# Attention, MLP and experts on one core: the first six attention groups in another order, with part of the first loads on ScalarE's DMA queue

## Chip, core and metric

The kernel runs on one core of a Trainium2 chip. The metric is device time in microseconds of one execution. The core has five engines that run their own instruction streams in order: TensorE (PE, with its weight loads PEld), VectorE (DVE), ScalarE (ACT), GpSimd (POOL) and SyncE (SP). DMAs are issued by an instruction on an engine's queue and carried out by 16 DMA engines; an engine that needs the data waits for a semaphore that the DMA raises when it has landed.

## What is computed

```python
# q, k, v: (2, 8, 576, 64); heads 0-3 local, heads 4-7 strided, stride 32
scores = np.where(mask, scale * q @ k.T, -1e9)
attn = softmax(scores)                     # row maximum taken off, sum + 1e-9
x = (attn @ v) -> (1152, 512)              # heads side by side
h = np.maximum(x @ w_in, 0.0)              # w_in (512, 2048)
x = h * h @ w_out                          # w_out (2048, 512)
p = domain_probs / (domain_probs.sum(-1, keepdims=True) + 1e-9)
out = sum(p[:, e:e+1] * (np.maximum(x @ w1[e], 0.0) @ w2[e]) for e in range(4))
```

## The kernel before

The work is cut into tasks: a DMA, a run of matmuls, one elementwise step. `Plan.add` records each with the engines that may run it and an estimated cost, the tasks it follows, the buffers that it takes and frees, and a rank. `Plan.run` then plays the tasks through a small model: whenever an engine is idle it takes the ready task of lowest rank, and the instructions are written out in the order of the model's start times. This order is fixed in the program; the hardware only waits on semaphores. Where TensorE would have nothing to do before a set point, the model puts in filler matmuls (128x512 on a zero tile, line 1395).

The attention is done in groups: `Strided(b, j)` (three per batch) and `Local(b, j)` (five per batch). `attend` (line 499) makes a group's tasks: loads of k, q and v; the scores, S (lines 404 to 408 and 471 to 479); row maximum, difference, Exp on ScalarE (line 537, or 531 for small groups), row sum, reciprocal, normalisation on GpSimd (line 541); four transposes, T (413, 483); a copy of them to SBUF on ScalarE (line 521); the values product, V (425, 493); and the split of the result into a high and a low part (ScalarE line 551, VectorE line 555) in the x tiles, which the MLP reads. T0, V0, T1 and so on name these steps of the group that comes first, second, ... in time on TensorE. Six groups of batch 0 (the list `startup`) stand at the start; the other ten are spread between MLP products later. V3 is the values product of the first `Local` group, the fourth.

The MLP's weights come as 8-byte words of which two 4-byte halves are fetched as `raw` (512 KB each) and put together on ScalarE (mid, line 695), VectorE (shift 698, low half 703), and split into a high part on ScalarE (line 709) and a low part on GpSimd or VectorE (line 713). The MLP's products (lines 732 to 734) are three matmuls of 384 columns each; the first of them needs x of the three strided groups and the first half of the first weight unit.

All loads are issued by SyncE, in the model's order. Tiles: k, q, v, p (probabilities), pt (their transposes), st (row statistics), raw, mid, val, w (weights); ba, bh, by are PSUM banks. `cb` holds masks and an identity in bf16 and is read by the first score matmul, `ident` (read from `ci`) by the transposes. The framework gives each DMA, whatever queue it is on, one of eight completion semaphores (DMAHW0 to DMAHW7) in turn, in the program's order, and makes it wait for the semaphore's previous DMA where that isn't known to be done.

Of the kernel before, what the change touches and what calls it, by code (L numbers as in the profile page):

```python
# [10 lines left out]
U32 = mybir.dt.uint32  # L11
# [57 lines left out]
class Plan:  # L69
# [10 lines left out]
    warm = 6900  # L80
# [23 lines left out]
    def run(self):  # L104
# [7 lines left out]
        ready = {"pe": [], "act": [], "dve": [], "pool": [], "dma": [], "none": []}  # L112
# [13 lines left out]
        while done < len(self.tasks):  # L126
# [4 lines left out]
            while events and events[0][0] == now:  # L131
# [6 lines left out]
                elif what == "end":  # L138
# [7 lines left out]
                    for y in then.get(t, ()):  # L146
                        waits[y] -= 1
                        lag = 0 if y.behind is t else self.DMA if t.ran == "dma" else self.SAME if t.ran in y.engines else self.CROSS
# [3 lines left out]
            for e in ready:  # L152
                while idle[e] and ready[e]:
# [21 lines left out]
                    got.end = now + got.engines[e] * (2 if e == "pe" and now < self.warm else 1)  # L175
                    order.append((now, len(order), got.emit, e))
# [18 lines left out]
def tile_attention_mlp_experts(ctx: ExitStack, tc: tile.TileContext, a, out):  # L195
# [24 lines left out]
    HOLD = 5500  # L220
    EACH = 3169
    AHEAD = 2080
    END2 = 13621
    END3 = 9597
    CONV0 = 7564
    CONV = 113841
# [5 lines left out]
    BASE = 3308  # L232
    R_MAX = 232
    R_EXP = 219
    R_NORM = 708
# [3 lines left out]
    R_LO = 383  # L239
    R_OUT = 2681  # L240
    GROUP = 4
    NRAW = 3
# [6 lines left out]
    LEAD0, LEAD = 8230, 2552  # L249
# [41 lines left out]
    def mm_r(n):  # L291
        return int(n / 2.4) + 13
# [13 lines left out]
    def dma(nbytes):  # L306
        return int(nbytes / 310) + 60
# [39 lines left out]
    t_cb = plan.add({"dma": dma(P * CB * 2)}, lambda e: nc.sync.dma_start(out=cb, in_=a["cb"]), rank=-10000)  # L347
    t_go = plan.add({"none": HOLD}, lambda e: None)
    t_ci = plan.add({"dma": dma(P * P * 4)}, lambda e: nc.sync.dma_start(out=ident, in_=a["ci"]), rank=4500)
# [21 lines left out]
    class Strided:  # L371
        def __init__(self, b, j):
# [6 lines left out]
            self.cost_s = mm_r(U * n) + 2 * U * packed(n, n)  # L379
# [12 lines left out]
        def load(self, env, what):  # L392
            b, n, c = self.b, self.n, self.r0 * 2 * NM
            if what == "k":
                nc.sync.dma_start(out=env["k"][:, : U * n], in_=a["ks"][b, :, c : c + U * n])
            elif what == "q":
                nc.sync.dma_start(out=env["q"][:, : U * n], in_=a["qs"][b, :, c : c + U * n])
            else:
                nc.sync.dma_start(out=env["v"], in_=a["vs"][b, self.j])
# [38 lines left out]
    class Local:  # L438
# [19 lines left out]
        def load(self, env, what):  # L458
            b, t0, nq = self.b, self.t0, self.nq
            if what == "k":  # L460
                nc.sync.dma_start(out=env["k"][:, : 2 * (STRIDE + nq)].rearrange("p (t c) -> p t c", t=2), in_=a["kl"][b, :, :, t0 : t0 + STRIDE + nq])
            elif what == "q":
                nc.sync.dma_start(out=env["q"][:, : 2 * nq], in_=a["ql"][b, :, 2 * t0 : 2 * (t0 + nq)])
# [1021 lines left out]
```

## Time and profile before

| what | us |
|---|---|
| median of 3 runs (625.24 to 626.15) | 625.48 |
| the profiled execution | 624.48 |
| its span, first to last instruction | 622.7 |
| TensorE busy in the span | 613.6 |

The profile is of one execution. A timeline row gives start, duration, engine, line, operation, and in brackets the idle time before it and what ended it. A windows row gives each engine's busy time in a stretch, the granted TensorE clock as a share of full speed (PEclk), the mean busy share of the 16 DMA engines and what they moved.

### The profile page before, as it was taken

What the parts mean: (1) busy time and instruction counts of PE and PEld (TensorE: products, weight loads), DVE (VectorE), ACT (ScalarE), POOL (GpSimd) and SP (SyncE); (2) the same over time, 40 slices, a digit from 0 to 9 for tenths busy, and PEclk for the clock granted to TensorE, in tenths of its full rate; (3) what the DMA queues carried; (4) which work ended last, traced back from release to release, by engine and by line L of the source; (5) the groups of instructions that cost most, each with busy time, mean ns of one, the idle gap of its engine ahead of it and who ended that gap; (6) DMA issues with size and microseconds to landing.
All of it is one profiled execution on the core that took longest, in us unless ns stands there. A gap on an engine that the chain in (4) does not pass through costs nothing.

```text
span 622.7 us, 10098 instructions
## 1 busy us (share of the span) xinstructions
PE 613.6 (99%) x3742; PEld 559.8 (90%) x3742; DVE 458.0 (74%) x883; ACT 298.9 (48%) x697; POOL 149.8 (24%) x170
## 2 busy tenths in 40 slices
PE   8999999999999999999999999999999999999997
PEld 4798999999899999999898989899898989898996
DVE  4688777887687994597767585867876775978654
ACT  2967684555453643475454444534444534444330
POOL 2332012544021101023223231404132231314000
PEclk9899999999999999999999999999999999999999
DMA  8977521122212200002030203020120302030012
GB/s 265 304 212 224 162 74 65 34 75 95 102 68 68 68 1 1 17 24 63 17 85 18 84 18 85 18 63 23 47 55 18 85 17 85 17 85 1 1 51 102
DMA packets 37441, 45.14 MB, mean 72 GB/s; under 512 B 4688, under 2 KB 26640, under 8 KB 37392
## 3 DMA queue, kind: packets, MB, share of 16 engines
q1 hardware_dynamic: 37392, 44.50, 23.4%
q8 instruction: 29, 0.48, 0.3%
q14 instruction: 20, 0.16, 0.1%
HBM read 42.13 MB, written 2.36 MB: 71 GB/s over the span
## 4 chain that ended last, share of the span: by engine, by line
PE 85%; DVE 8%; ACT 2%; issue 2%; DMA 2%; SPq 1%; DVEq 0%; ACTq 0%
PE by L1247 11%; PE by L1246 11%; PE by L1248 10%; PE bh L732 10%; PE bh L733 10%; PE bh L734 10%; PE by L732 3%; PE by L734 3%; PE by L733 3%; PE ba L732 3%; PE ba L733 3%; PE ba L734 3%; DVE r L971 1%; PE ba L479 1%; DMA raw<-in_wi_dram 1%
## 5 line engine op out<-in xcount | busy, mean ns | idle before, releaser
L1199 DVE SCALAR_TENSOR_TENSOR acc<-by,pe,acc 128x512 f32<-128x512 f32 (+1 forms) x109 | 79.2, 742 | 24.5 <-PE by L1248 24.2
L732 PE MATMUL bh<-x,w 128*128 128x384 f32 x240 | 82.8, 345 | 0.7 <-DVE h L1271 0.4
L733 PE MATMUL bh<-x,w 128*128 128x384 f32 x240 | 80.6, 336 | 0.2 <-DVE x L767 0.2
L734 PE MATMUL bh<-x,w 128*128 128x384 f32 x240 | 80.5, 336 | 0.0
L1144 POOL TENSOR_TENSOR sf<-raw,raw 128x256 f32<-128x256 f32 x40 | 32.0, 804 | 183.6 <-DMA raw<-in_w_dram 133.2
L1155 ACT ACTIVATE w<-sf 128x256 fp32r<-128x256 f32 x110 | 43.4, 409 | 50.6 <-POOL sf L1144 50.6
L1247 PE MATMUL by<-o,h 128*128 128x512 f32 (+1 forms) x134 | 52.4, 391 | 0.0
L1246 PE MATMUL by<-o,h 128*128 128x512 f32 (+1 forms) x134 | 52.1, 389 | 0.0
L1248 PE MATMUL by<-o,h 128*128 128x512 f32 (+1 forms) x134 | 51.8, 386 | 0.0
L732 PE MATMUL by<-h,w 128*128 128x384 f32 x144 | 49.7, 345 | 1.0 <-ACT acc L837 1.0
L732 PEld LDWEIGHTS bh<-x,w 128*128 128x128 f32 x240 | 45.2, 188 | 4.0 <-DVE r L1366 1.1
L734 PE MATMUL by<-h,w 128*128 128x384 f32 x144 | 48.3, 335 | 0.0
L733 PE MATMUL by<-h,w 128*128 128x384 f32 x144 | 48.2, 335 | 0.0
L733 PEld LDWEIGHTS bh<-x,w 128*128 128x128 f32 x240 | 45.2, 188 | 1.0 <-DVE x L767 0.5
L734 PEld LDWEIGHTS bh<-x,w 128*128 128x128 f32 x240 | 45.1, 188 | 0.0
L1144 POOL TENSOR_TENSOR sf<-sf,raw 128x256 f32<-128x256 f32 x40 | 32.3, 817 | 22.4 <-DVE w L1163 22.2
L733 PE MATMUL bh<-w,w 128*128 128x384 f32 x110 | 37.0, 336 | 0.0
L734 PE MATMUL bh<-w,w 128*128 128x384 f32 x110 | 36.9, 336 | 0.0
L732 PE MATMUL bh<-w,w 128*128 128x384 f32 x110 | 36.9, 335 | 0.0
L1179 DVE TENSOR_TENSOR o<-raw,o 128x512 fp32r<-128x512 f32 x30 | 21.1, 706 | 21.3 <-ACT o L1176 21.3
L1176 ACT ACTIVATE o<-raw 128x512 fp32r<-128x512 f32 x30 | 18.8, 631 | 35.9 <-PE by L1248 35.5
L1366 DVE TENSOR_TENSOR r<-r,bh 128x384 f32<-128x384 f32 x49 | 26.9, 550 | 11.4 <-ACT r L1361 7.1
(268 smaller groups left out, 1627.9 us busy)
## 6 DMA issues: line engine op xcount, KB each, us to landing
raw<-in_wi_dram SPq DMA_DIRECT2D x16, 512.0 KB, 3.9
raw<-in_wo_dram SPq DMA_DIRECT2D x16, 512.0 KB, 3.9
raw<-in_w_dram SPq DMA_DIRECT2D x64, 128.0 KB, 2.7
raw<-in_w_dram SPq DMA_DIRECT2D x32, 256.0 KB, 2.8
out_dram<-acc SPq DMA_DIRECT2D x8, 256.0 KB, 2.0
v<-in_vs_dram SPq DMA_DIRECT2D x6, 256.0 KB, 4.4
v<-in_vl_dram SPq DMA_DIRECT2D x8, 192.0 KB, 4.1
k<-in_kl_dram SPq DMA_DIRECT2D x8, 160.0 KB, 4.1
```

Of the source, the lines that this page charges most:

```text
L732: nc.tensor.matmul(dst, lhsT=wh, rhs=xh, start=start, stop=False, skip_group_check=again)
L733: nc.tensor.matmul(dst, lhsT=wh, rhs=xl, start=False, stop=False, skip_group_check=again)
L734: nc.tensor.matmul(dst, lhsT=wl, rhs=xh, start=False, stop=stop, skip_group_check=again)
L1144: nc.gpsimd.tensor_tensor(out=value(dst), in0=value(x), in1=value(y), op=ALU.subtract if n in MINUS else ALU.add)
L1155: nc.scalar.activation(out=op_slot(env["op"])[:, 0].rearrange("p k f -> p (k f)"), in_=value(src), func=AF.Copy, scale=float(sign))
L1176: nc.scalar.activation(out=late[env["w2"]][:, 0], in_=f32(raws[f]["raw"][:, DM:]), func=AF.Copy)
L1179: nc.vector.tensor_tensor(out=late[env["w2"]][:, 1], in0=f32(raws[f]["raw"][:, DM:]), in1=f32(late[env["w2"]][:, 0]), op=ALU.subtract)
L1199: nc.vector.scalar_tensor_tensor(out=acc, in0=o, scalar=pcol, in1=acc, op0=ALU.mult, op1=ALU.add)
L1246: nc.tensor.matmul(o, lhsT=h[:, 0, ts], rhs=w[:, 0], start=new, stop=False)
L1247: nc.tensor.matmul(o, lhsT=h[:, 0, ts], rhs=w[:, 1], start=False, stop=False)
L1248: nc.tensor.matmul(o, lhsT=h[:, 1, ts], rhs=w[:, 0], start=False, stop=stop)
L1366: nc.vector.tensor_tensor(out=at_(), in0=at_(), in1=bank["bank"][:, :TB], op=ALU.add if sign > 0 else ALU.subtract)
```

## The change

DMAs may now stand on a second queue, "dma2", issued by ScalarE (`nc.scalar.dma_start`); the model lets the two queues share the rate, and all "dma2" tasks are written out at time 0. On it go `cb`, `ident`, the v of the first six groups and the first two raw weight tiles; all other loads stay on SyncE. The six groups have ranks of their own (FIRST, LKQ, LV), and for them the copy of the transposes, the high part of the result and the normalisation may also run on VectorE; the high part of the first weight units may too. The first four MLP products have ranks of their own (EARLY_H) and may use the banks `by`. Some constants of the planner are other numbers.

```diff
-    warm = 6900
+    warm = 5300
...
-                    order.append((now, len(order), got.emit, e))
+                    other = {"dma": "dma2", "dma2": "dma"}.get(e)
+                    slow = now < self.warm if e == "pe" else other and (ready[other] or not idle[other])
+                    got.end = now + got.engines[e] * (2 if slow else 1)
+                    order.append((0 if e == "dma2" else now, len(order), got.emit, e))
...
-    HOLD = 5500
-    EACH = 3169
+    HOLD = 4721
...
+    FIRST = (-15498, -14603, 1146, 17685, 23706, 17552)
+    LKQ = (-9194, -10361, -8349, -7854, -7681, -7609)
+    LV = (-9957, -8431, -7025, -8031, -5968, -3705)
...
+    AHEAD_H = 4
+    EARLY_H = (-14744, -12844, 22108, 24008), (-6663, -4763, 42744, 44644), (21457, 23357, 48317, 50217), (-34452, -32552, 21056, 22956)
...
+    QUEUE2 = (("wi", 0, 1), ("wi", 0, 0))
...
-    t_cb = plan.add({"dma": dma(P * CB * 2)}, lambda e: nc.sync.dma_start(out=cb, in_=a["cb"]), rank=-10000)
+    t_cb = plan.add({"dma2": dma(P * CB * 2)}, lambda e: nc.scalar.dma_start(out=cb, in_=a["cb"]), rank=-10000)
...
-            loads.append(plan.add({"dma": dma(nbytes)}, lambda e, w=what: g.load(env, w), rank=rank - lead, take=[(env, what, [what])]))
+            loads.append(plan.add({"dma2" if early is not None and what == "v" else "dma": dma(nbytes)}, lambda e, w=what: g.load(env, w, nc.scalar if e == "dma2" else nc.sync), rank=(LV if what == "v" else LKQ)[early] if early is not None else rank - lead, take=[(env, what, [what])]))
...
-        t = plan.add({"pool": norm(n)}, lambda e: eng[e].tensor_tensor(out=view(env["p"]), in0=view(env["p"]), in1=wide(1), op=ALU.mult), after=[t], rank=rank + R_NORM, free=[(env, "st")])
+        t = plan.add({"pool": norm(n), "dve": dve(n)} if early is not None else {"pool": norm(n)}, lambda e: eng[e].tensor_tensor(out=view(env["p"]), in0=view(env["p"]), in1=wide(1), op=ALU.mult), port=True, after=[t], rank=rank + R_NORM, free=[(env, "st")])
...
-        t = plan.add({"act": act(g.npt)}, copy, after=[t], rank=rank + R_T + 500, take=[(env, "pt", ["pt"])], free=[(env, "T")])
+        t = plan.add({"act": act(g.npt), "dve": dve(g.npt)} if early is not None else {"act": act(g.npt)}, copy, after=[t], rank=rank + r_t + 500, take=[(env, "pt", ["pt"])], free=[(env, "T")])
...
-            t = plan.add({"act": act(cols)}, hi, after=[t_v], rank=rank + R_X)
+            t = plan.add({"act": act(cols), "dve": dve(cols)} if early is not None else {"act": act(cols)}, hi, after=[t_v], rank=rank + r_x)
...
-        attend(g, BASE + EACH * k, ["bank_a", "bank_y"], LEAD0)
+        attend(g, FIRST[k], ["bank_a", "bank_y"], 0, k, WHOLE[k])
...
-                chain["dma"] = plan.add({"dma": dma(P * 4 * CH * 4)}, load, after=[chain["dma"]], rank=rank - FETCH, take=[(env, "raw", ["raw"])])
+                chain["dma"] = plan.add({"dma2" if (kind, c, j) in QUEUE2 else "dma": dma(P * 4 * CH * 4)}, load, after=[chain["dma"]], rank=LW.get((kind, c, j), rank - FETCH), take=[(env, "raw", ["raw"])])
```

What this makes of the program's order at three places (names as in the code, with buffer numbers; the sizes are partitions x elements).

SyncE's first DMAs before:

```order
L347 DMA cb<-in_cb_dram 128x410
L395 DMA k_115<-in_ks_dram 128x432
L397 DMA q_111<-in_qs_dram 128x432
L399 DMA v_119<-in_vs_dram 128x512
L395 DMA k_116<-in_ks_dram 128x432
L397 DMA q_112<-in_qs_dram 128x432
L399 DMA v_120<-in_vs_dram 128x512
L395 DMA k_117<-in_ks_dram 128x288
L397 DMA q_113<-in_qs_dram 128x288 [waits DMAHW0_49]
L399 DMA v_121<-in_vs_dram 128x512 [waits DMAHW1_49]
L349 DMA ident<-in_ci_dram 128x128 [waits DMAHW2_49]
```

And after, on the same queue, with the semaphores that each waits for:

```order
L407 DMA k_115<-in_ks_dram 128x432
L409 DMA q_111<-in_qs_dram 128x432
L407 DMA k_116<-in_ks_dram 128x432
L409 DMA q_112<-in_qs_dram 128x432
L407 DMA k_117<-in_ks_dram 128x288
L409 DMA q_113<-in_qs_dram 128x288 [waits DMAHW1_49]
L473 DMA k_118<-in_kl_dram 128x2x160 [waits DMAHW3_49]
L475 DMA q_114<-in_ql_dram 128x256 [waits DMAHW5_49]
```

SyncE has k and q alone at the start; the second strided group's now come first. ScalarE's queue before, from its start:

```order
L537 ACT_TABLE_LOAD
L537 ACTIVATE p_125<-p_125 128x8x54 [waits DVE_49]
L537 ACTIVATE p_126<-p_126 128x8x54 [waits DVE_49]
L537 ACTIVATE p_127<-p_127 128x8x36 [waits DVE_49]
L521 ACTIVATE pt_130<-by_108 128x512 [waits PE_49]
```

And after, from its start:

```order
L411 DMA v_119<-in_vs_dram 128x512
L708 DMA raw_90<-in_wi_dram 128x1024
L361 DMA ident<-in_ci_dram 128x128 [waits DMAHW0_49]
L411 DMA v_120<-in_vs_dram 128x512 [waits DMAHW2_49]
L708 DMA raw_91<-in_wi_dram 128x1024 [waits DMAHW4_49]
L477 DMA v_121<-in_vl_dram 96x512 [waits DMAHW7_49]
L411 DMA v_122<-in_vs_dram 128x512 [waits DMAHW1_49]
L477 DMA v_123<-in_vl_dram 96x512 [waits DMAHW2_49]
L477 DMA v_124<-in_vl_dram 96x512 [waits DMAHW3_49]
L550 ACT_TABLE_LOAD
L550 ACTIVATE p_125<-p_125 128x8x54 [waits DVE_49]
L714 ACTIVATE mid_93<-raw_90 128x512
```

The DMA of `cb` stands ahead of these, without a wait. The ten DMAs stand ahead of the table load and the first Exp. VectorE before, from its first row maximum (L526) on:

```order
L526 TENSOR_REDUCE st_132<-ba_105 128x8
L536 TENSOR_TENSOR p_125<-ba_105,st_132 128x8x54
L526 TENSOR_REDUCE st_133<-ba_106 128x8
L536 TENSOR_TENSOR p_126<-ba_106,st_133 128x8x54
L538 TENSOR_REDUCE st_132<-p_125 128x8
```

And after:

```order
L539 TENSOR_REDUCE st_132<-ba_105 128x8
L549 TENSOR_TENSOR p_125<-ba_105,st_132 128x8x54
L551 TENSOR_REDUCE st_132<-p_125 128x8
L717 TENSOR_SCALAR val_95<-mid_93 128x512
L552 TENSOR_SCALAR st_132<-st_132 128x8
L722 SCALAR_TENSOR_TENSOR val_95<-raw_90,val_95 128x512
L539 TENSOR_REDUCE st_133<-ba_106 128x8
L553 RECIPROCAL st_132<-st_132 128x8
L549 TENSOR_TENSOR p_126<-ba_106,st_133 128x8x54
```

The sum of the first group's Exps (L538 before, L551 after) and two steps of the first weight's conversion now stand ahead of the second group's maximum. On TensorE the first MLP products stand earlier among the attention steps, right behind V3 and one set of transposes:

```order
L505 MATMUL ba_105<-pt_131,v_121 64x64 x8
L495 MATMUL by_107<-ident,p_129 96x128 x4
L754 MATMUL bh_103<-x_75,w_80 128x384
L755 MATMUL bh_103<-x_75,w_80 128x384
L756 MATMUL bh_103<-x_75,w_80 128x384
L754 MATMUL bh_104<-x_75,w_80 128x384
```

Before, a score and two sets of transposes stood there, and the MLP products were taken one at a time. From the matmul after the last attention group's values product on, both kernels have the same order on TensorE.

## Rows read from the trace of the kernel before

**Rows 1.** The page, part 1: busy us (share of span), instructions.
```profile
PE 613.6 (99%) x3742; PEld 559.8 (90%) x3742; DVE 458.0 (74%) x883; ACT 298.9 (48%) x697; POOL 149.8 (24%) x170
```
**Rows 2.** Windows: length, busy us by engine (instructions), PEclk, DMA share, GB/s.
```profile
100.00:150.00 50.00, 49.90 (x297) 49.51 (x294) 41.19 (x63) 25.86 (x53) 23.10 (x19) 1.00 0.20 64
```
**Rows 3.** TensorE's timeline: start us, duration us, operation, idle before and releaser.
```profile
5.65 0.57 PE L404 MATMUL ba<-cb 128*128 128x432 bf16 x1
...
11.28 0.88 PE L479 MATMUL ba<-k,q 64*64 64x96 f32 x16 [1.07 <-DMA q<-in_ql_dram]
...
14.30 0.60 PE L413 MATMUL by<-ident,p 128*128 128x128 f32 x4
...
15.17 0.60 PE L413 MATMUL by<-ident,p 128*128 128x128 f32 x4
...
21.69 0.69 PE L493 MATMUL by<-pt,v 96*64 96x64 f32 x16
23.22 0.38 PE L474 MATMUL ba<-cb 128*128 128x384 bf16 x1 [0.84 <-DVE x L555]
...
26.60 0.50 PE L732 MATMUL bh<-x,w 128*128 128x384 f32 x1
...
99.66 0.69 PE L493 MATMUL ba<-pt,v 96*64 96x64 f32 x16
```
**Rows 4.** Windows, the stretch of the lower clock.
```profile
23.35:26.76 3.41, 3.41 (x26) 2.94 (x26) 2.56 (x10) 2.68 (x8) 2.06 (x2) 0.50 1.04 408
```
**Rows 5.** ScalarE's timeline.
```profile
0.73 1.28 ACT L537 ACT_TABLE_LOAD   x1 [0.73 <-PEq L1474]
8.61 0.56 ACT L537 ACTIVATE p<-p 128x432 f32<-128x432 f32 x1 [6.59 <-DVE p L536]
...
15.63 0.68 ACT L695 ACTIVATE mid<-raw 128x512 f32<-128x512 f32 x1
```
**Rows 6.** SyncE's DMA issues in its timeline.
```profile
1.18 0.42 SPq L395 DMA_DIRECT2D k<-in_ks_dram  x1
...
3.06 0.43 SPq L397 DMA_DIRECT2D q<-in_qs_dram  x1
...
7.72 0.34 SPq L465 DMA_DIRECT2D v<-in_vl_dram  x1
```
**Rows 7.** SyncE's waits: total us, times, longest.
```profile
SPq L465 <- DMA q<-in_qs_dram: 0.5, 1, 0.5
```
**Rows 8.** Windows, the rate of the loads (the last two numbers of a row).
```profile
0.00:5.00 5.00, 4.01 (x10) 1.49 (x11) 0.11 (x1) 1.28 (x1) 2.57 (x9) 1.00 0.56 165
5.00:10.00 5.00, 4.54 (x104) 2.92 (x101) 2.23 (x4) 0.56 (x1) 0.00 (x0) 1.00 0.98 321
10.00:15.00 5.00, 3.93 (x46) 2.57 (x45) 3.79 (x15) 1.07 (x3) 1.78 (x2) 1.00 1.07 307
...
25.00:30.00 5.00, 5.00 (x58) 4.25 (x57) 3.48 (x12) 4.06 (x17) 1.41 (x2) 0.82 1.03 393
```
**Rows 9.** The chain of waits, first 30 us: start, us from issue to landing.
```profile
3.06 4.64 DMA q<-in_qs_dram
...
10.16 5.46 DMA raw<-in_wi_dram
```
**Rows 10.** The tile k, first 30 us: its twelve DMAs.
```profile
DMA to landing us min/median/max: 2.8/4.1/6.0
```
**Rows 11.** VectorE's timeline: difference, sum, and a weight's shift and low half.
```profile
9.59 0.61 DVE L536 TENSOR_TENSOR p<-ba,st 128x432 f32<-128x432 f32 x1
10.12 0.59 DVE L538 TENSOR_REDUCE st<-p 128x8 f32<-128x432 f32 x1
...
16.34 0.43 DVE L698 TENSOR_SCALAR val<-mid 128x512 uint32<-128x512 uint32 x1 [1.02 <-ACT mid L695]
16.80 0.69 DVE L703 SCALAR_TENSOR_TENSOR val<-raw,val 128x512 uint32<-128x512 uint32 x1
```
**Rows 12.** GpSimd's timeline: the normalisations of the first two groups.
```profile
11.92 1.78 POOL L541 TENSOR_TENSOR p<-p,st 128x432 f32<-128x432 f32 x2 [8.82 <-DVE st L539]
```

More of the change, by code (lines that the diff above doesn't have):

```diff
@@ L147, in run @@
                         waits[y] -= 1
-                        lag = 0 if y.behind is t else self.DMA if t.ran == "dma" else self.SAME if t.ran in y.engines else self.CROSS
+                        lag = 0 if y.behind is t else self.DMA if t.ran in ("dma", "dma2") else self.SAME if t.ran in y.engines else self.CROSS
                         ready_at[y] = max(ready_at.get(y, 0), now + lag)
@@ L500, in tile_attention_mlp_experts, with attend @@
     attention_done, transposed = [], []
-    def attend(g, rank, rings, lead):
+    def attend(g, rank, rings, lead, early=None, whole=False):
         env = {}
+        r_t, r_v, r_x = ((S_T, S_V, S_X) if g.kk == (2, 3) else (L_T, L_V, L_X)) if early is not None else (R_T, R_V, R_X)
         n = g.units * g.cols
@@ L526, in attend @@
         t = plan.add({"dve": dve(n)}, lambda e: nc.vector.tensor_reduce(out=stat(0), in_=view(env["S"], g.cols), op=ALU.max, axis=AX.X), after=[t], rank=rank + R_MAX, take=[(env, "st", ["st"])])
-        if g.units <= 4:
+        if g.units <= 4 and not whole:
             def each(e):
@@ L680, in tile_attention_mlp_experts @@
         wide_ = kind in ("wi", "wo")
-        soon = wide_ and first[u] <= LAG
-        rank = when[u] - (CONV0 if soon else CONV2 if not wide_ else CONV if c <= half // 2 else CONV1)
+        soon = wide_ and c == 0
+        rank = when[u] - (CONV2 if not wide_ else CONV if c <= half // 2 else CONV1)
+        late_ = rank
         for j in (1, 0) if kind == "wi" else (0, 1):
+            rank = EARLY.get((kind, c, j), late_) if wide_ else late_
             env = {} if wide_ or j == 0 else env
@@ L688, in load @@
                 if wide_:
-                    nc.sync.dma_start(out=env["raw"], in_=a[kind][k].bitcast(U32))
+                    (nc.scalar if e == "dma2" else nc.sync).dma_start(out=env["raw"], in_=a[kind][k].bitcast(U32))
                 else:
@@ L708, in hi @@
             def hi(e, u=u, cs=cs, value=value):
-                nc.scalar.activation(out=weights(u)[:, 0, cs], in_=value(), func=AF.Copy)
+                if e == "act":
+                    nc.scalar.activation(out=weights(u)[:, 0, cs], in_=value(), func=AF.Copy)
+                else:
+                    nc.vector.tensor_copy(weights(u)[:, 0, cs], value())
             def lo(e, u=u, cs=cs, value=value):
@@ L722, in tile_attention_mlp_experts @@
                 t = plan.add({"dve": dve(n)}, low, port=True, after=[t], rank=rank + 1200, free=[(env, "raw")])
-            t = plan.add({"act": act(n)}, hi, after=[t, chain["w"]], rank=rank + 2000, take=[(w_env[u], "w", ["w"])] if u not in w_ready else [], quiet=not wide_)
+            t = plan.add({"act": act(n), "dve": dve(n)} if soon else {"act": act(n)}, hi, after=[t, chain["w"]], rank=rank + 2000, take=[(w_env[u], "w", ["w"])] if u not in w_ready else [], quiet=not wide_)
             chain["w"] = t
```

66 lines of the change are left out of this document (37 added, 29 removed).

## Prediction

> **What bounds the kernel now.** I read the page's busy table first: TensorE is busy 99% of the span [rows 1]. Then the windows: from 100 to 150 us it is busy 49.90 of 50 us [rows 2], and for 28 to 100 us the view of its waits names none. So the time is TensorE's work plus what it loses before that work runs without gaps, and only the head of the trace can change much. The reader should see three losses in TensorE's timeline [rows 3]. The first 5.65 us are eleven filler matmuls ahead of the first data. Between there and 22.4 us stand short waits, 1.07 us for a q the longest, and eight more fillers. Then, after the values product V3 (21.69 + 0.69 = 22.38), TensorE stands 0.84 us, and the granted clock falls: 0.50 for the 3.41 us from 23.35, the lower of its two levels, 1.2 GHz [rows 4]. At half speed that stretch cost about 1.7 us. The first product of the MLP starts at 26.60.
>
> From the matmul after the last attention product on (99.66 us [rows 3]) the changed kernel has the same TensorE order as before. So I ask only: by how much earlier or later does TensorE get there?
>
> **The order before.** ScalarE's first Exp starts at 8.61 [rows 5]; its table load stood at 0.73 and was long done. SyncE issues everything, one DMA per 0.47 us (four from 1.18 to 3.06 [rows 6]). Every DMA takes one of eight completion semaphores in turn and waits until the DMA eight places ahead of it has landed; the view of SyncE's waits shows one such wait, 0.5 us for a q [rows 7], on a queue that has nothing else to do.
>
> **What the change adds: ScalarE waits on DMAs.** Ten DMAs now stand on ScalarE's own queue ahead of its table load and its first Exp. Their issue alone costs little: 10 x 0.47 = 4.7 us from 0.73, then 1.28 us for the table load [rows 5, 6], ends at 6.7, before the first Exp is wanted (8.61). That alone I cost at nothing. But seven of the ten wait for a semaphore, and the semaphores are shared with SyncE's DMAs. Counted in the program's order, the last one (v_124) waits for the lane of SyncE's seventh DMA, the k of group 3, and v_123 waits for the second v. SyncE may issue that k only after its own first q has landed. So ScalarE is held until those have landed, and VectorE's row sum of the first group, TensorE's transposes and all behind them wait for that Exp.
>
> When do they land? The windows give 165, 321 and 307 GB/s for the first three 5 us, so 0.82, 2.43 and 3.97 MB by 5, 10 and 15 us [rows 8]. Two landings calibrate it: the second q (the sixth DMA, 1.25 MB summed, moved by 6.3) lands at 3.06 + 4.64 = 7.70, and the first raw weight (3.64 MB, moved by 13.9) at 10.16 + 5.46 = 15.62 [rows 9]. So a landing comes about 1.5 us after its bytes' turn. Up to that k SyncE carries 1312 KB and ScalarE, up to the second v, 1190 KB.
> - In order of issue: 2502 KB = 2.56 MB, moved by 10.4, landed 11.9.
> - With equal shares for both queues: 2 x 1312 KB = 2.69 MB, moved by 10.8, landed 12.3.
> - One DMA of each queue in turn: ScalarE's first seven (1894 KB) go along, 3206 KB = 3.28 MB, moved by 12.8, landed 14.3.
> - At the least: that q is the third DMA to land, 0.55 MB, moved by 3.3, landed 4.8 with the same lag; no k landed in under 2.8 us [rows 10], so 7.6.
>
> Behind the landing come the last issue (0.34 to 0.43 us [rows 6]) and the table load (1.28), 1.7 us with gaps. The first Exp then starts at 13.6, 14.0 or 16.0, and not before 9.3. I take 14.0, since neither queue has a reason to be served first: **5.4 us later** than 8.61, bounds +0.7 to +7.4.
>
> **Is the rest of the chain shorter?** From the first Exp to the end of V3, before: 22.38 - 8.61 = 13.8 us. After, with X for the Exp's start: VectorE now has the row sum, then two steps of the weight conversion (shift 0.43, low half 0.69, behind ScalarE's 0.68 for mid), and only then the second group's maximum 0.61 and difference 0.61 [rows 5, 11]. ScalarE's mid ends at X + 1.2, the low half at X + 2.3, the difference at X + 3.5, so the second Exp starts at X + 3.55. The first group's normalisation on GpSimd (1.78 for two, 0.89 each [rows 12]) follows the reciprocal, T0 at X + 4.0 (before: 14.30, X + 5.7, since fillers and a score stood ahead). The second group: sum, the copy of T0 (now VectorE's; about 0.6, my estimate from the low half's 0.69 for the same 512 columns), two small steps and the third group's sum, reciprocal at X + 6.3. GpSimd's normalisation then gives T1 at X + 7.6 (before X + 6.6). From T1 to V3's end the same copies, casts and products follow, in before 7.2 us from T1 at 15.17; now V1 waits for T1's copy on ScalarE, and T3 and V3 for VectorE's multiplication and ScalarE's Exps. I take 6.0, since the q and raw loads that held that stretch before (1.07 us for a q [rows 3], raw at 15.62) have landed by then. The chain is 13.6 us long: **-0.2**, bounds -2.0 and +1.0.
>
> **After V3.** Four MLP products of three matmuls now stand right behind V3 and one transpose, with their weights ready, so the 0.84 us are saved: **-0.8**. The clock: TensorE will stand or fill for some 4 us before T0, longer than any wait before, so I expect it to fall again, at a price like the 1.7 us of before: **0** net, bounds -1.7 (it holds) and +2 (it stays low through a part of the chain from T0 to V3, which holds some 8 us of matmuls). From 28 to 100 us the order differs (attention groups and MLP products change places); TensorE has no gap there now, so it can only get some: **+0.5**, bounds 0 and +1.5. Six casts of attention results, two copies and three normalisations go to VectorE, 0.2 to 0.7 us each; they lie in the chain above. With v gone from it, SyncE's queue runs through the first k and q sooner; nothing is late there.
>
> **Sum.** 5.4 - 0.2 - 0.8 + 0 + 0.5 = +4.9 us. The profiled execution took 624.48 (span 622.7); 629.4 against that, and the median of the runs shown, 625.48, lies 1.0 above it: **630.4**. With the Exp at 13.6 to 14.6 and the clock's bounds its own range is 628 to 633.
>
> **Rivals.**
> 1. *The lanes clear early; faster.* If the second queue lets that k and the second v land near the least time, the first Exp starts by 10.1. With X = 9.6: +1.0 - 0.2 - 0.8 - 1.7 (the wait before T0 is then too short for the clock to fall) = -1.7, **623.8**. It decides at the first Exp: before 10.1 faster by over 0.2%. For it: the engines moved 393 GB/s at 25 to 30 us [rows 8]. Against it: they were already busy with one queue's packets from 2 us on. By the Trainium skill (DMA: Bandwidth & Descriptors, section Issuing engines are not separate DMA queues) issuing from several engines saves only issue time, which would leave this rival no more bandwidth; no run here shows two queues yet. Chance 0.13.
> 2. *Late, but paid back; within 0.2%.* At 393 GB/s from 2 us on, 2.69 MB are moved by 8.8 and landed at 10.3, the Exp starts at 12.0: +3.4 - 0.2 - 0.8 - 1.7 = +0.7, **626.2**. It needs both the rate and a clock that holds. Chance 0.12.
> 3. *The queues alternate by whole DMAs; slower still.* The first Exp starts at 16.0: +7.4 - 0.2 - 0.8 + 0 + 0.5 = +6.9, **632.4**. For it: ScalarE's DMAs are the larger ones (up to 512 KB against 216), so turns cost SyncE more than half. The Trainium skill (same page, section Queues, rings and completion order) says that each DMA engine goes round the queues packet by packet, a packet being some 9 to 17 descriptors; that would be this case. No row here has two queues in flight. Chance 0.20.
>
> **How the numbers follow.** My forecast (slower, about +4.9) has 0.55, rival 3 has 0.20, rival 1 has 0.13, rival 2 has 0.12. A measurement of this kernel can tell about 0.2% (1.25 us) from no change: 624.2 to 626.7 counts as the same. Faster 0.13, same 0.12, slower 0.75. The range 624.5 to 634.0 takes in rival 2, the forecast and rival 3, and leaves out most of rival 1 and a longer fall of the clock, under 0.2 together.
>
> **What would show it.** Right: in the profile after, ScalarE's first Exp near 14 us with its table load just before, its queue waiting for DMAs of k and v; VectorE idle from about 8.6 to then; T0 near 18; the first MLP product at 27 to 29; the last attention product 4 to 5 us later than 99.66. Wrong: the table load by 7 us or the first Exp by 10 (then the lanes don't hold, rival 1); a first Exp as forecast but no gap before T0 (the chain is shorter than I have it); gaps of TensorE after 100 us, where the orders agree.

## The result, and the profile after

The changed kernel takes **628.53 us** (median of 6 runs, 628.08 to 629.22) against 625.36 us before (6 runs beside them, 624.93 to 627.12): **1.0052**, 95% interval 1.0035 to 1.0068. The forecast was 630.4 us, 4.9 above the 625.48 known then. The profiled execution of after is its 629.03 one, with a span of 627.2; that of before (624.48) had 622.7. So the two traces differ by 4.5 us and the medians by 3.2: the traced execution of before took 0.9 us less than its median, that of after 0.5 us more. The traces are compared here.

ScalarE first. It issues the ten DMAs, then comes what it did at 0.73 and 8.61 before [rows 5]:

```profile
4.25 0.34 ACTq L361 DMA_DIRECT2D ident<-in_ci_dram  x1
...
9.79 0.81 ACTq L477 DMA_DIRECT2D v<-in_vl_dram  x2
10.64 1.28 ACT L550 ACT_TABLE_LOAD   x1 [10.64 <-DMA k<-in_kl_dram]
11.93 0.56 ACT L550 ACTIVATE p<-p 128x432 f32<-128x432 f32 x1
...
15.49 0.56 ACT L550 ACTIVATE p<-p 128x432 f32<-128x432 f32 x1 [0.60 <-DVE p L549]
```

The chain of waits (start us, length us, what) names the landings that held the issues, two in a row: the second v waits for the landing of the first at 5.31, and itself lands at 9.77. The issue of 9.79 is v_123, the last but one:

```profile
1.17 4.14 DMA v<-in_vs_dram
5.31 0.02 issue
5.33 4.44 DMA v<-in_vs_dram
9.77 0.02 issue
9.79 0.34 ACTq L477
10.13 0.04 issue
10.17 0.44 ACTq L477
10.61 0.03 issue
10.64 1.28 ACT L550
```

The loads came faster than with one queue [rows 8]. Windows of after with SyncE alone (length, PEclk, DMA share, GB/s):

```profile
2.00:4.00 2.00, 1.00 0.92 296
4.00:6.00 2.00, 1.00 1.05 406
6.00:8.00 2.00, 1.00 1.04 378
8.00:10.00 2.00, 1.00 1.01 268
```

TensorE's timeline, to be read against [rows 3]: T0 after a stand of 4.14 us, V3, the first MLP product, a wait for VectorE, the last attention product, and a wait that came after it:

```profile
15.97 1.12 PE L425 MATMUL ba<-ident,p 128*128 128x128 f32 x4 [4.14 <-POOL p L554]
...
26.86 0.69 PE L505 MATMUL ba<-pt,v 96*64 96x64 f32 x16
...
28.02 0.42 PE L754 MATMUL bh<-x,w 128*128 128x384 f32 x1
...
84.35 0.44 PE L754 MATMUL bh<-x,w 128*128 128x384 f32 x1 [0.84 <-DVE h L825]
...
102.73 0.69 PE L505 MATMUL ba<-pt,v 96*64 96x64 f32 x16
...
157.52 0.44 PE L754 MATMUL bh<-x,w 128*128 128x384 f32 x1 [1.29 <-DVE val L904]
```

Windows of TensorE (length, busy us, PEclk, DMA share, GB/s) show the lower clock inside the chain, where [rows 4] had it behind V3. Its exact stretch is 14.54 to 21.37, 6.8 us; behind V3 it does not fall again.

```profile
14.00:16.00 2.00, 0.03 (x1) 0.64 1.09 245
16.00:18.00 2.00, 2.00 (x11) 0.50 1.05 334
18.00:20.00 2.00, 2.00 (x34) 0.50 0.39 126
20.00:22.00 2.00, 2.00 (x37) 0.66 0.00 0
```

Three marks divide the difference. V3 ends at 26.86 + 0.69 = 27.55 (before 22.38): +5.2. Up to there both kernels have done the same matmuls, but for eight more fillers in after. The last attention product starts at 102.73 (before 99.66): +3.1. The span ends 4.5 us later.

Behind this second mark TensorE's order is not quite the same, other than the section on the change and the prediction have it: 2688 matmuls follow it in before and 2691 in after. One MLP product, three matmuls or 0.5 us at the 0.17 us at which they follow each other, has moved behind the mark, and the orders agree only from some 60 us behind it. At equal work after is therefore 3.1 + 0.5 = 3.6 us late at the mark: 1.6 us are given back between the first two marks, and **0.9 us are lost after the second mark, where the prediction expected nothing**. TensorE's stands there (the time it is idle between matmuls) add up to 3.03 us in after and 2.17 in before, which is these 0.9 us. The larger ones are the 1.29 us above, for VectorE, and these for ScalarE; two fences, before and after:

```profile
158.04 0.44 PE L732 MATMUL by<-h,w 128*128 128x384 f32 x1 [0.42 <-ACT acc L837]
161.46 0.45 PE L732 MATMUL by<-h,w 128*128 128x384 f32 x1 [0.53 <-ACT acc L837]
```
```profile
163.65 0.44 PE L754 MATMUL by<-h,w 128*128 128x384 f32 x1 [0.64 <-ACT acc L859]
```

### The profile page after: what moved, and what is told of

It reads as the page before. It is cut to its first block, busy times and chain, and to the rows that moved or that the text cites. A ratio compares the mean times of both kernels' runs of the same rounds, so it can differ in the third digit from the quotient of the medians.

```text
span 627.2 us, 10110 instructions
## 1 busy us (share of the span) xinstructions
PE 614.7 (98%) x3750; PEld 560.6 (89%) x3750; DVE 459.8 (73%) x891; ACT 293.9 (47%) x688; POOL 150.7 (24%) x171
## 4 chain that ended last, share of the span: by engine, by line
PE 88%; DVE 6%; issue 2%; DMA 1%; ACT 1%; POOL 0%; ACTq 0%; DVEq 0%; POOLq 0%
PE bh L754 11%; PE by L1269 11%; PE by L1268 11%; PE by L1270 10%; PE bh L755 10%; PE bh L756 10%; PE by L754 4%; PE by L756 4%; PE by L755 4%; PE ba L754 3%; PE ba L756 3%; PE ba L755 3%; DMA v<-in_vs_dram 1%; PE ba L491 1%; DVE r L993 1%
## 5 line engine op out<-in xcount | busy, mean ns | idle before, releaser
L754 PE MATMUL bh<-x,w 128*128 128x384 f32 x230 | 78.8, 343 | 2.6 <-DVE val L904 1.3
L755 PE MATMUL bh<-x,w 128*128 128x384 f32 x230 | 77.2, 336 | 0.2 <-DVE x L789 0.2
L756 PE MATMUL bh<-x,w 128*128 128x384 f32 x230 | 77.1, 335 | 0.0
L1177 ACT ACTIVATE w<-sf 128x256 fp32r<-128x256 f32 x110 | 42.1, 406 | 34.0 <-POOL sf L1166 34.0
L754 PEld LDWEIGHTS bh<-x,w 128*128 128x128 f32 x230 | 43.1, 188 | 5.8 <-DVE val L904 1.6
L755 PEld LDWEIGHTS bh<-x,w 128*128 128x128 f32 x230 | 43.2, 188 | 1.0 <-DVE x L789 0.5
L756 PEld LDWEIGHTS bh<-x,w 128*128 128x128 f32 x230 | 43.2, 188 | 0.0
```

Of the source, the lines that this page charges most:

```text
L754: nc.tensor.matmul(dst, lhsT=wh, rhs=xh, start=start, stop=False, skip_group_check=again)
L755: nc.tensor.matmul(dst, lhsT=wh, rhs=xl, start=False, stop=False, skip_group_check=again)
L756: nc.tensor.matmul(dst, lhsT=wl, rhs=xh, start=False, stop=stop, skip_group_check=again)
L1177: nc.scalar.activation(out=op_slot(env["op"])[:, 0].rearrange("p k f -> p (k f)"), in_=value(src), func=AF.Copy, scale=float(sign))
```

## Experiments

The first Exp, V3's end and the last attention product (written L) can be read in every kernel's trace; "rest" is the span less L. Times are medians; each was set beside runs of before on its own chip (medians 625.1 to 625.4). These columns but the last two are of one execution each. The diffs are against the changed kernel unless another is named, and show of a long line only the part that changes.

| kernel | first Exp | V3 ends | clock falls before V3 | L | rest | median us | ratio to before, interval |
|---|---|---|---|---|---|---|---|
| before | 8.61 | 22.38 | no (behind V3) | 99.66 | 523.0 | 625.36 | |
| after | 11.93 | 27.55 | yes | 102.73 | 524.5 | 628.53 | 1.0052 (1.0035 to 1.0068) |
| e1_table | 14.98 | 29.72 | yes | 104.89 | 527.2 | 635.65 | 1.0166 (1.0149 to 1.0183) |
| e2_fill | 13.14 | 31.32 | yes | 106.48 | 524.6 | 633.64 | 1.0142 (1.0126 to 1.0158) |
| e3_planned | 7.75 | 23.32 | no | 98.45 | 524.6 | 625.43 | 1.0005 (0.9987 to 1.0022) |
| e4_three | 7.90 | 22.62 | no | 98.25 | 524.7 | 624.39 | 0.9990 (0.9981 to 0.9999) |
| e5_warm | 12.49 | 26.00 | no | 101.18 | 524.6 | 627.79 | 1.0038 (1.0022 to 1.0054) |
| e6_eight | 11.38 | 24.89 | no | 100.06 | 524.6 | 627.97 | 1.0041 (1.0028 to 1.0055) |
| e7_onequeue | 8.45 | 23.15 | no | 98.33 | 524.5 | 624.01 | 0.9984 (0.9970 to 0.9998) |
| e8_split | 8.11 | 22.92 | no | 98.10 | 522.6 | 622.42 | 0.9958 (0.9942 to 0.9974) |
| e9_after_split | 13.29 | 28.93 | yes | 104.08 | 522.6 | 627.74 | 1.0047 (1.0031 to 1.0062) |
| e10_before_split | 8.11 | 24.26 | yes, and behind V3 | 101.57 | 522.6 | 624.95 | 0.9995 (0.9983 to 1.0006) |
| e11_one_split | 8.81 | 22.33 | no | 97.50 | 522.6 | 622.02 | 0.9961 (0.9945 to 0.9976) |
| e12_five_split | 8.24 | 22.44 | no | 97.63 | 522.8 | 622.18 | 0.9955 (0.9939 to 0.9970) |

### Are the lane waits on ScalarE the loss? e4_three, e3_planned, e7_onequeue, e6_eight

**e4_three.** The DMAs are emitted at their planned time, and only cb, the first v and the first raw weight go through ScalarE:

```diff
-order.append((0 if e == "dma2" else now, len(order), got.emit, e))
+order.append((now, len(order), got.emit, e))
-lambda e: nc.scalar.dma_start(out=ident, in_=a["ci"])
+lambda e: nc.sync.dma_start(out=ident, in_=a["ci"])
-g.load(env, w, nc.scalar if e == "dma2" else nc.sync)
+g.load(env, w, nc.scalar if e == "dma2" and early == 0 else nc.sync)
-(nc.scalar if e == "dma2" else nc.sync).dma_start(out=env["raw"], ...
+(nc.scalar if (kind, k) == ("wi", 1) else nc.sync).dma_start(out=env["raw"], ...
```

> The changed kernel with three DMAs on ScalarE (cb, the first v, the first raw weight), none of which has to wait for a lane; the other seven go through SyncE where the plan's time puts them among the k and q. Theory (lane waits on ScalarE are the loss): table load at 2.1, first Exp at 8.0 to 8.6, wait before T0 under 1.5 us, time 624 to 625.5. Rival a (order of groups and VectorE's work cost by themselves): time above 626.5 in spite of an early Exp. Rival b (the two queues together brought 400 GB/s from 4 to 6 us against 269 before; with seven DMAs back on SyncE's queue the loads are late again): ident, q or v late by 1 to 3 us, TensorE waits for a DMA ahead of T0 or V0, time 625.5 to 627.

Measured 624.39. ScalarE's and TensorE's timelines (two fences):

```profile
2.14 1.28 ACT L550 ACT_TABLE_LOAD   x1 [2.14 <-issue]
7.90 0.56 ACT L550 ACTIVATE p<-p 128x432 f32<-128x432 f32 x1 [4.47 <-DVE p L549]
```
```profile
12.84 0.60 PE L425 MATMUL ba<-ident,p 128*128 128x128 f32 x4
...
21.93 0.69 PE L505 MATMUL ba<-pt,v 96*64 96x64 f32 x16 [0.21 <-issue]
...
98.25 0.69 PE L505 MATMUL ba<-pt,v 96*64 96x64 f32 x16
```

The table load is done by 3.4, the Exp waits for VectorE alone, T0 has no wait, the clock stays at 1.00, and L is 4.5 us earlier than in after with the same order of groups and the same VectorE work. The theory holds, and rival a falls: up to L that order is 1.4 us earlier than before, 0.9 us at equal work.

**e3_planned** has the first of these edits alone: five DMAs ahead of the table load, five among ScalarE's activations.

```diff
-order.append((0 if e == "dma2" else now, len(order), got.emit, e))
+order.append((now, len(order), got.emit, e))
```

> The changed kernel with ScalarE's DMAs issued where the plan's time puts them, instead of all ten ahead of everything: five (cb, v, raw, ident, v) stay ahead of the table load, the other five (raw and four v) stand between ScalarE's first eight activations. SyncE's order is as in the changed kernel. Theory (ten DMAs with lane waits ahead of the first Exp are the whole loss): table load done by 7, first Exp at 8.0 to 8.6, wait before T0 under 1.5 us, time 624 to 625.5. Rival a (the new order of groups and VectorE's work are slower by themselves): first Exp just as early, but the time stays above 626.5. Rival b (a new wait takes its place): raw or a v, now in the middle of ScalarE's work, waits for its lane and holds the second or third Exp; first Exp near 8.5, second at 13 or later, time 626.5 to 628.

Measured 625.43 (623.59 to 628.51, the widest spread of the variants), profile at 624.82. The first Exp is at 7.75, a little ahead of what was expected, and rival b's wait is there too, later than expected (the second Exp is at 11.32): a v holds ScalarE until 14.57, and V3 stands for ScalarE's copy.

```profile
14.57 0.35 ACTq L411 DMA_DIRECT2D v<-in_vs_dram  x1
14.96 0.67 ACT L714 ACTIVATE mid<-raw 128x512 f32<-128x512 f32 x1 [1.95 <-DMA q<-in_ql_dram]
```
```profile
22.63 0.69 PE L505 MATMUL ba<-pt,v 96*64 96x64 f32 x16 [1.03 <-ACT pt L534]
```

The clock does not fall in this trace, but its twelve executions divide as those of e6_eight below do: seven with a mean granted clock of 0.999 or 1.000 took 623.59 to 626.52, five at 0.995 to 0.997 took 625.83 to 628.51.

**e7_onequeue** is e3_planned with every DMA on SyncE (v as below; cb, ident and raw in the same way).

```diff
-g.load(env, w, nc.scalar if e == "dma2" else nc.sync)
+g.load(env, w, nc.sync)
```

> The changed kernel with all its DMAs on SyncE, in the order of the plan's times; the order of groups, VectorE's additional work and the later part as in the changed kernel. It separates the second queue from the rest; to be set beside e4_three (three DMAs on ScalarE, first Exp 7.90, 624.4). Theory (the second queue's use is small next to the lane waits): first Exp at 8 to 9, no clock fall, time 624 to 625.5. Rival (the second queue brings the first loads sooner): scores, first Exp and T0 each 1 us or more later than in e4_three, a DMA wait of TensorE of over 1 us, time 625.5 to 627.

Measured 624.01: the second queue is worth nothing here. It does move more at first. Windows of all engines (the last number is GB/s), e4_three and then e7_onequeue:

```profile
2.00:4.00 2.00, 2.00 (x7) 0.66 (x5) 0.00 (x0) 1.28 (x1) 1.10 (x3) 1.00 0.95 301
4.00:6.00 2.00, 2.00 (x26) 0.96 (x26) 0.00 (x0) 0.00 (x0) 0.00 (x0) 1.00 1.02 391
```
```profile
2.00:4.00 2.00, 2.00 (x7) 0.66 (x5) 0.00 (x0) 0.02 (x1) 1.10 (x3) 1.00 0.79 216
4.00:6.00 2.00, 1.87 (x6) 0.55 (x4) 0.00 (x0) 0.00 (x0) 0.00 (x0) 1.00 0.98 339
```

One queue brings the second q later (TensorE stands 1.18 us for it at 10.25, 0.95 in e4_three), but both Exps come from VectorE in time and L differs by 0.1. By the Trainium skill (DMA: Bandwidth & Descriptors, section Issuing engines are not separate DMA queues) a second issuing engine saves only issue time; the equal times agree with that, and the higher rate stands in the first microseconds, while few DMAs have been issued.

**e6_eight** takes the last two v off ScalarE and leaves the lanes ahead of them as they were.

```diff
-order.append((0 if e == "dma2" else now, len(order), got.emit, e))
+order.append((0 if e == "dma2" and got.rank not in (-5968, -3705) else now, len(order), got.emit, e))
-g.load(env, w, nc.scalar if e == "dma2" else nc.sync)
+g.load(env, w, nc.scalar if e == "dma2" and early not in (4, 5) else nc.sync)
```

> The changed kernel with eight DMAs instead of ten on ScalarE: the last two (the v of the fifth and sixth group, the two that wait for the second v and for the k of group 3) go through SyncE at their planned time, behind its first raw weight. The lanes of everything before them are as in the changed kernel. Theory (each lane wait on ScalarE moves the first Exp, and with it the end): the last issue ends at 9.5 instead of 10.6, first Exp at 10.9 instead of 11.93, T0 near 14.9, time 1.0 to 2.3 below 628.5: 626.2 to 627.5 (e1_table, where the first Exp came 3.05 later, was 7.1 slower: 2.3 per us). Rival (the clock falls as soon as TensorE stands at all, at a fixed price): the time is at most 0.5 below, 628.0 or more.

Measured 627.97, above the expected range; the profile is the fastest of its twelve executions (626.48). In it the first Exp is at 11.38, the stand before T0 3.07 us, and the clock does not fall; L is 2.7 us earlier than in after. Its executions divide by their mean granted clock: two at 1.000 took 626.48 and 627.67, seven at 0.996 or 0.997 took 627.47 to 628.06, three at 0.995 took 628.70 to 629.20. Where in those executions the clock fell no trace shows. The median itself lies 0.6 below after, between theory and rival, and decides nothing.

```profile
10.09 1.28 ACT L550 ACT_TABLE_LOAD   x1 [10.09 <-DMA v<-in_vs_dram]
11.38 0.57 ACT L550 ACTIVATE p<-p 128x432 f32<-128x432 f32 x1
```
```profile
15.42 0.66 PE L425 MATMUL ba<-ident,p 128*128 128x128 f32 x4 [3.07 <-POOL p L554]
...
24.20 0.69 PE L505 MATMUL ba<-pt,v 96*64 96x64 f32 x16 [0.38 <-ACT pt L534]
```

### The price of the clock: e5_warm, e2_fill

**e5_warm**: sixteen fillers ahead of T0 (`early == 1`; e2_fill had `early == 0`).

```diff
-lambda e: g.transposes(env), after=[t, t_ci]
+lambda e: ([warm(e) for _ in range(16 if early == 1 else 0)], g.transposes(env)), after=[t, t_ci]
```

> The changed kernel with sixteen more filler matmuls on TensorE ahead of T0 itself (run e2_fill had them one transposes step later, ahead of T1). Theory (the clock's fall doubles a part of the chain behind T0): with the clock at 1.0 the stretch from the first Exp to V3's end takes about 13.6 us instead of 15.6, and the time is 1 to 2.5 us below the changed kernel's 628.5: 626 to 627.5. Rival a (ScalarE, VectorE and GpSimd bound that stretch): it still takes 15 us or more, the time is 628 to 628.5. Rival b (the fall is only put off): the clock falls behind V3 or inside the chain in spite of the fillers, and the time is 628 or more. The first Exp may itself lie anywhere from 11.9 to 13.1, as in the changed kernel and e2_fill; the stretch is counted from it.

```profile
12.49 0.56 ACT L550 ACTIVATE p<-p 128x432 f32<-128x432 f32 x1
```
```profile
11.45 4.28 PE L1417 MATMUL by<-idle 128*128 128x512 bf16 x19
16.54 0.66 PE L425 MATMUL ba<-ident,p 128*128 128x128 f32 x4 [0.81 <-POOL p L554]
...
25.31 0.69 PE L505 MATMUL ba<-pt,v 96*64 96x64 f32 x16 [0.38 <-ACT pt L534]
```

From the first Exp to V3's end: 26.00 - 12.49 = 13.51 us, and 24.89 - 11.38 = 13.51 in e6_eight, against 27.55 - 11.93 = 15.62 in after. **The fall costs 2.1 us in this trace.** The Exp itself came 0.56 later, so L gains 1.55; the time is 627.79, 0.3 above the top of the expected range, and its ratio's interval overlaps that of after.

That trace of after is not a typical one. Its mean granted clock is 0.995, with 6.8 us at the lower clock; the other five executions have 0.997, which is the mean of before's trace with its 3.4 us. So 2.1 us is the price in the profiled execution; in the others the fall should be shorter and cost less, but no trace of one was kept. Nor does the clock fall in every execution of before: of the 72 that ran beside the experiments, 32 have a mean of 0.999 or 1.000 and a median of 624.3 us, 40 have 0.992 to 0.997 and a median of 625.6.

**e2_fill** was meant as this run, but its fillers stood ahead of T1 and not of T0.

> The changed kernel with sixteen more filler matmuls (bf16, 512 columns) on TensorE right ahead of T0, where it stood 4.14 us; they need no data and end before T0's input is there. Theory (half of the chain's lengthening, 15.6 us from the first Exp to V3's end instead of 13.6, is the granted clock of 0.50 from 14.54 to 21.37): the clock is 1.0 through T0 to V0, V3 ends 1 to 2.5 us earlier than 27.55, the time is 626 to 627.5. Rival a (the chain is bound by ScalarE, VectorE and GpSimd; TensorE's speed is hidden): the clock holds, V3 ends within 0.5 us of 27.55, the time is 628.0 to 628.5. Rival b (the fall is only put off): the clock falls behind V3 as in the kernel before (0.50 for 3.4 us from 23.35), and the time is 628 or more.

Measured 633.64. The clock fell before they ran, and they took 3.63 us from 22.53 in the middle of the chain (Exp to V3's end 18.2); L is 3.75 later than in after. It tells nothing of the clock, only that this chain hides no work of TensorE.

### An early table load: e1_table

```diff
-lambda e: nc.scalar.dma_start(out=ident, in_=a["ci"])
+early_exp = const.tile([P, 8], F32, name="early_exp")
+lambda e: (nc.scalar.activation(out=early_exp, in_=idle[:, :8], func=AF.Exp), nc.scalar.dma_start(out=ident, in_=a["ci"]))
```

> The changed kernel with one small Exp (8 columns of a constant) on ScalarE ahead of its fourth DMA, where ScalarE waits from 2.1 to 4.2 us in any case; so the 1.28 us table load no longer stands between the last lane wait and the first Exp. Everything else as in the changed kernel. Theory (ScalarE's lane waits set the first Exp, and the chain hangs on it): table load near 2.1, first Exp at 10.6 instead of 11.93, T0 at 14.7 instead of 15.97, and the time 1.3 us below the changed kernel's 628.5, so 627.2; to 626.2 if the shorter wait also shortens the low clock. Rival (the first Exp is not what the chain waits for; the new order of groups and VectorE's additional work are): T0 stays within 0.3 us of 15.97 and the time at 628.5.

Measured 635.65, the wrong way. With one more instruction the program's order of DMAs on the two queues changed, so the eight semaphores were dealt out differently (ident now waits for the first q instead of cb, and others of both queues changed too), and the waits grew; ident and the second v are issued 1.0 and 3.3 us later than in after:

```profile
5.29 0.34 ACTq L362 DMA_DIRECT2D ident<-in_ci_dram  x1
8.60 0.36 ACTq L412 DMA_DIRECT2D v<-in_vs_dram  x1
...
14.98 0.56 ACT L551 ACTIVATE p<-p 128x432 f32<-128x432 f32 x1 [11.34 <-DMA v<-in_vs_dram]
```

So it is no test of the table load, but a third point for the price of a late Exp. Only 2.2 of its 4.9 us (of span) lie before L; the other 2.7 come evenly after 300 us and are left open below. The slope of 2.3 per us that e6_eight's expectation took from it is therefore wrong.

Put together, for the order of after: with the clock held, L goes from 98.3 (Exp at 7.9 or 8.45) to 100.06 (11.38) and 101.18 (12.49), and the last step is 1 us for 1. Carried to 11.93 that is 100.6. **So of after's 102.73, 2.3 us come from the late Exp and 2.1 from the clock**; e9_after_split (13.29, clock fell) lies 2.1 above the same line too, e1_table 1.2. The division is good to some 0.5 us: with the Exp at 7.75 to 8.81 six traces have L at 97.5 to 98.5.

### The loss after 100 us: e8_split, e9_after_split, e10_before_split

In after a multiplication on VectorE (L993, the square r = mid * mid; the expectations below call it a subtraction), 0.55 us elsewhere, takes 2.42 and ends at 155.52, 0.41 behind GpSimd's sum of two weight halves (155.11). Two fences, VectorE and GpSimd:

```profile
153.10 2.42 DVE L993 TENSOR_TENSOR r<-mid 128x384 f32<-128x384 f32 x1
```
```profile
152.72 2.39 POOL L686 TENSOR_TENSOR raw<-w 128x1024 f32<-128x1024 f32 x1 [3.89 <-issue]
```

In before the same pair met with the tail of the sum only, and the square (L971 there) again ends 0.42 behind it (151.86 and 151.44):

```profile
150.47 1.39 DVE L971 TENSOR_TENSOR r<-mid 128x384 f32<-128x384 f32 x1 [0.59 <-ACT mid L968]
```
```profile
149.05 2.39 POOL L670 TENSOR_TENSOR raw<-w 128x1024 f32<-128x1024 f32 x1
```

**e8_split** is e4_three with that sum in four pieces:

```diff
-nc.gpsimd.tensor_tensor(out=f32(env["raw"]), in0=w[:, 0], in1=w[:, 1], op=ALU.add)
+for i in range(4):
+    part_ = slice(i * CH, (i + 1) * CH)
+    nc.gpsimd.tensor_tensor(out=f32(env["raw"])[:, part_], in0=w[:, 0, part_], in1=w[:, 1, part_], op=ALU.add)
```

> e4_three with GpSimd's sum of two weight halves (128 x 1024) in four instructions of 256 columns instead of one of 2.4 us; nothing else is moved. In e4_three, as in the changed kernel, VectorE's subtraction at 148.64 took 2.42 us instead of 0.56 and ended with that sum (148.26 to 150.65), and TensorE then stood 1.30 us for VectorE at 153.07. Theory (VectorE's instruction waits for the end of GpSimd's; that is a loss of the changed plan that has nothing to do with the queues): the subtraction takes under 1.3 us, the 1.30 us wait falls to 0.3 or less, time 1.0 below e4_three's 624.4: 623.2 to 623.7. Rival (VectorE is slow there for another reason, or waits through all four pieces): the subtraction stays over 2 us, the time at 624.4.

Measured 622.42, 2.0 below e4_three, twice what was expected, and 0.4% below before. The square takes 0.72 us beside the pieces, and the wait of 1.3 us is gone:

```profile
148.38 0.72 DVE L995 TENSOR_TENSOR r<-mid 128x384 f32<-128x384 f32 x1
```

The Trainium skill (SBUF — State Buffer, section SBUF: two separate sides) has this as an exclusive lock: VectorE with two inputs in SBUF and a GpSimd instruction that reads SBUF share a pair of ports, and the one that comes second waits for the other's whole instruction. Both inputs of the square are the SBUF tile mid, the sum reads w, and the sum had started first (152.72, 153.10). The 2.42 us that end just behind the sum, and the 0.72 beside pieces, agree.

**e9_after_split**, the edit in the changed kernel itself:

> The changed kernel with the edit of e8_split alone (GpSimd's sum of two weight halves in four instructions); the ten DMAs on ScalarE stay. In e8_split, with three DMAs there, the sum in pieces took 2.0 off (624.39 to 622.42). Theory (the losses at the head and at 150 us are independent and add up): the wait of 1.29 us for VectorE at 157.5 is gone, the head is as in the changed kernel, time 628.5 - 2.0 = 626.5. Rival (a later start at the head hides or changes the collision): the time stays within 0.7 of 628.5.

Measured 627.74: 0.8 below after, not 2.0, and the intervals overlap. The trace says where it went: the rest after L is 522.6 instead of 524.5, the 1.29 us wait is gone, but in this execution the first Exp came at 13.29 and L 1.35 later. The same ten DMAs gave 11.93, 13.14, 12.49 and 13.29 in four traces. And four of its five executions have a mean clock of 0.995, against one of after's six. The head varies by nearly as much as the edit is worth.

**e10_before_split**, the edit in the kernel before:

> The kernel before with the same edit of GpSimd's sum. There the sum ran from 149.05 to 151.44 and VectorE's subtraction took 1.39 us from 150.47 (0.56 elsewhere); TensorE then stood 0.42 and 0.53 us for ScalarE's acc. Theory (before meets the same collision, but only its tail, and pays less for it): 0.4 to 0.9 below 625.3, so 624.4 to 624.9. Rival (the sum in pieces is good for any order, by as much as in e8_split): 623.3. Second rival (before does not pay for it at all): 625.3.

Measured 624.95, no difference that can be told. In the trace, the slowest of its twelve, the rest after L falls from 523.0 to 522.6, the theory's 0.4, but not where the theory put it: the square still takes 1.11 us and the stand of 0.42 behind it is 0.68 here; set side by side matmul by matmul, the gain comes near 120 and 189 us. **In after's order the four kernels with the sum in pieces have a rest of 522.6 to 522.8, whatever their head, and the seven with it whole 524.5 to 524.7 (e1_table apart); in before's order it is 522.6 and 523.0.** So the whole sum costs after's order 1.9 us (1.5 to 1.6 of them at this pair, matmul by matmul) and before's 0.4. That difference of 1.5 us is more than the 0.9 lost at equal work; the changed order makes up the rest by fewer other waits (with the sum in pieces TensorE stands 1.55 us behind L in e9_after_split and 2.35 in e10_before_split).

### A version that beats both: e11_one_split, e12_five_split

Both are e8_split with another share of the queues: e11_one_split has all DMAs on SyncE as in e7_onequeue, e12_five_split also has ident and the second v on ScalarE.

> e7_onequeue (all DMAs on SyncE in the planned order, the changed kernel's order of groups) with the edit of GpSimd's sum. Theory (second queue worth nothing, the two edits add): 624.0 - 2.0 = 622.0, the same within 0.5 as e8_split's 622.4. Rival (the three DMAs on ScalarE help once the later wait is gone): 622.9 or more.

Measured 622.02 (e7_onequeue and e8_split's edit): the two add.

> e8_split with five DMAs on ScalarE (cb, first v, first raw weight, ident, second v) instead of three; ident and the second v there wait for a lane, as in e3_planned, where the table load came at 5.54 and the first Exp at 7.75. The raw weight and four v that held ScalarE's third and fourth step in e3_planned go through SyncE. Theory (lane waits cost only what they add behind the time at which VectorE has the first Exp's input, about 7.7): first Exp at 7.7 to 7.9, T0 at 11.8 to 12.8, time 621.4 to 622.4. Rival (any lane wait on ScalarE costs): first Exp at 8.5 or later in some executions, time 623 or more.

```diff
-g.load(env, w, nc.scalar if e == "dma2" and early == 0 else nc.sync)
+g.load(env, w, nc.scalar if e == "dma2" and early in (0, 1) else nc.sync)
-lambda e: nc.sync.dma_start(out=ident, in_=a["ci"])
+lambda e: nc.scalar.dma_start(out=ident, in_=a["ci"])
```

Measured 622.18, with the first Exp 0.3 us later than expected. ident and the second v wait for lanes on ScalarE, but are issued by 5.7, ahead of what the first Exp (8.24) needs. e8_split, e11_one_split and e12_five_split cannot be told from each other; all three are 0.4% faster than before.

## Why the prediction was right, and where it was not

- **ScalarE held by the lanes.** Right, and shown: v_123 waits for the second v, as counted, and without the waits (e4_three, e7_onequeue) the loss is gone. Five issues ahead of the Exp, two of them with a wait, cost nothing that can be told (e12_five_split).
- **When they land: +5.4.** The mis-sized term: the first Exp moved by 3.3 us (11.93, not 14.0), inside the bounds. The landing came at 9.77 and not at 12.3. I took one queue's rate, 321 GB/s from 5 us on; with two queues the windows of after (last number, below the chain in the first section) show 296, 406 and 378 GB/s for 2 to 8 us and 268 behind, and 2.69 MB are moved by 9.8 us, not 10.8. The other 1.5 us of the landing lie in the 1.5 us of lag or in the equal shares; these runs do not separate them. What the trace shows in place of a count of bytes is two landings in a row, 4.14 and 4.44 us. Behind the landing stood two issues and not one, so that the Exp followed it by 2.2 us, not 1.7. Other executions of the same ten DMAs had 12.5 to 13.3.
- **The rest of the chain: -0.2.** Right with the clock held: 13.51 us (e5_warm, e6_eight) where I had 13.6, so -0.3, the second Exp at X + 3.56, T0 at X + 4.04.
- **After V3: -0.8.** Right: products follow V3 without a gap.
- **The clock: 0 net.** Between the traces it came to +0.4, in two parts: +2.1 inside the chain, at the upper bound I gave, and -1.7 because the fall behind V3 [rows 4] did not come again. The -1.7 is the prediction's estimate, and what is given back between V3 and L bears it out: 1.6 us at equal work, while TensorE's stands there are nearly the same (0.86 us before, 0.99 after).
- **Later gaps, up to 100 us: +0.5.** What is left at L is 3.6 - (3.3 - 0.3 - 0.8 + 0.4) = +1.0, inside the bounds, and TensorE's stands from V3 to L are 0.99 us, 0.84 of them at 84.35.
- **After 100 us: nothing.** This step failed: "So I ask only: by how much earlier or later does TensorE get there?" It came to +0.9. TensorE's order is not the same, by one product, and the plan also moved GpSimd's sum against VectorE's work, which costs it 1.5 us more than before. The prediction named gaps there as a sign that it was wrong, and the 1.29 us at 157.52 is one; it had not looked at those two engines.

Sum: 3.3 - 0.3 - 0.8 + 0.4 + 1.0 + 0.9 = +4.5, the difference of the spans. That the forecast's +4.9 lies so near is luck: the Exp had 2.1 us too much, and the clock, the later gaps and the part after 100 us together 1.8 too little. Against the medians (+3.2) it is 1.7 too much. Of the rivals, 2 had the Exp nearly right (12.0) by a rate that was too high (2.69 MB by 8.8 us, measured 9.8) and a landing that was too late, and was wrong on the clock. Rival 1's case can be seen in e4_three and e7_onequeue: with the Exp before 10 the changed order gains about 1 us, and 2.8 to 3.1 where the sum is in pieces too (e8_split, e11_one_split), so the collision takes back some 2 us of what the head gives. Rival 3 fell: no Exp came at 16. The rule that it cites, turns packet by packet, is also not one of turns by whole DMAs, from which it has its 16 us; the equal shares of the forecast are nearer to it.

## What to carry to other kernels

Here a DMA issued from ScalarE cost it not only the 0.4 us of issue but the landing of whatever its semaphore waited for: ten of them held the first Exp until 11.93, three without a wait let it start at 7.90. List for each such DMA which landing that is, and put on a computing engine only those that are clear before its first arithmetic is wanted. When a plan's numbers move, compare the order of every engine over the whole kernel, not that of the bottleneck alone, and count the work on both sides of a mark before calling two orders the same. A long GpSimd instruction that falls beside VectorE's critical one can be worth cutting into pieces (2.0 us here, e8_split; 0.4 in before's order).

## What the runs showed of the hardware that I had not expected

- VectorE's multiplication of 0.55 us took 2.42 beside one GpSimd instruction of 2.39 us, 0.72 beside pieces of it.
- Two queues moved 301 and 391 GB/s from 2 to 6 us, one queue 216 and 339, with no gain in time.
- TensorE stood 4.14 us and its clock fell (after), stood 3.07 and it held (e6_eight), stood 0.84 behind V3 and it fell (before): the length of the stand alone does not decide.
- e1_table ran slower from 300 us on with the same instructions: from one SyncE DMA issue (L623, there L624) to another it took 566.25 - 322.91 = 243.3 us, in after 561.93 - 320.48 = 241.5. It has one more tile of 32 bytes per partition ahead of the others; whether that is the cause was not tried.
